# Attention and squared-ReLU MoE on one core: loading w_out once, with a scale for each of its rows

## The chip, the cores and the metric

The kernel runs on one core of a Trainium2 chip (trn2). The metric is the device time of one execution in microseconds (us), lower is better. Before the change the runs gave a median of 1171.84 us (3 runs, 1171.61 to 1176.66).

## The reference, cut to what matters

```python
# q, k, v: (8, 8, 576, 64) float32; w_in (512, 2048), w_out (2048, 512), both float64
scores = (1 / np.sqrt(64)) * np.matmul(q, k.transpose(0, 1, 3, 2))
mask = block_i >= block_j                       # blocks of 64 positions
scores = np.where(mask, scores, -1000000000.0)
scores = scores - np.max(scores, axis=-1, keepdims=True)
attn = np.exp(scores)
attn = attn / (np.sum(attn, axis=-1, keepdims=True) + 1e-09)
attn_out = np.matmul(attn, v)
x = attn_out.transpose(0, 2, 1, 3).reshape(4608, 512)
h = x @ w_in
r = np.maximum(h, 0.0)
return ((r * r) @ w_out).astype(np.float32)
```

## The kernel before, in words

**Attention.** The 8 heads of each of 8 batches are taken in 4 pairs. A "pass" is one pair on some of its 9 blocks of 64 queries. Passes 0 to 7 do the first three blocks of batches 0 and 1, passes 8 to 11 the other six blocks of batch 0, passes 12 to 15 those of batch 1, and passes 16 to 39 all nine blocks of batches 2 to 7. A pass computes the scores (`ps`, L406), the softmax (`nmx`, `p`, `rs`, `p_rows`, L425 to L456), turns the probabilities (`p_turned`) and multiplies them by v (`px`, L537). Up to pass 11 TensorE turns them (`pt`, L486, evicted at L488); from pass 12 on two DMA transposes for each pass do (L459, queued on SyncE), into one buffer, and probabilities and v are split into two f16 parts (`p_rows` z = 0 and 1, L454 and L455; `v`, L377 and L378).

**MoE.** The tokens go in 12 chunks of 384. A chunk has 16 hidden units `ph` of 12 matmuls each (`moe_in`, L685), whose relu (`r`, L692) is squared into an f16 pair (`g`, L694 to L696), and three outputs `po` of 48 matmuls each (`moe_out`, L711, 144 in all), evicted to `ob` (L719) and stored. TensorE's f16 products need each float64 weight as a scaled f16 pair `w1h`, `w1l` (w_in) and `w2h`, `w2l` (w_out).

**The weights.** The 16 tiles of w_in (512 KB each) are loaded once, early on; `weight_scale(0)` takes a maximum over each group of 4 tiles, and `weight_parts(0)` makes the pair. For w_out, `weight_scale(1)` loads all 16 tiles (named `wa`), reduces each to a maximum for every partition (L265) and then takes one maximum over all; after that `weight_parts(1)` loads all 16 tiles a second time (named `wb`) and splits them: ScalarE's Prelu (L305), VectorE's shift and or (L307, L308), ScalarE's cast to `w2h` (L309), GpSimd's rest to `w2l` (L310). All these tiles take their buffers from the ring of three that the q and k tiles of the passes use too (tag `qk32`, L218).

**What sets the order.** The program emits one pass after another (`one_pass`) and between the groups of a pass pours in steps of generators (`fill`): `first_moe` for chunk 0, then `moe` for each chunk that is complete. In `first_moe` one step is a hidden unit, together with a tile of w_in's parts and, from unit 8 on, one `wa` tile; when the 16 units are out, `wb` tiles and then `moe_out` follow. `load` of the pass after next stands at the end of a pass, `load_v` three passes ahead, into a ring of four `vraw` buffers. All loads, stores and transposes are issued by SyncE in one queue (SP). The tile scheduler then moves instructions of one engine by its own estimate, so that each engine's final order is not that of the code.

Of the kernel before, what the change touches and what calls it, by code (L numbers as in the profile page):

```python
# [58 lines left out]
BP = 99  # L59
BS = 99  # L60
# [39 lines left out]
def attention_moe_kernel(ctx: ExitStack, tc: tile.TileContext, qkt, vm, vt, w_in, w_out, out):  # L100
# [16 lines left out]
    vraw = [const.tile([P, 2, 5, D], F32, name=f"vraw{i}") for i in range(4)]  # L117
# [120 lines left out]
    gate = {}  # L238

    wsc = [const.tile([P, n], F32, name=f"wsc{i}") for i, n in enumerate((NG, 1))]  # L240
    wm = const.tile([P, NG], F32, name="wm")

# [13 lines left out]
    def weight_scale(wi):  # L256
# [3 lines left out]
        tok, ng = ((tokA, NG), (tokB, 1))[wi]  # L260
        st = small.tile([P, NF], F32, tag="stw", name=f"stw_{wi}", bufs=1)
        n = NF // ng
        for f in range(NF):
            _, _, hf = load_w(w_out, f, f"wa{wi}_{f}") if wi else w1raw[f]
            i = nc.vector.tensor_reduce(st[:, f : f + 1], hf, axis=AX.X, op=ALU.max, apply_absolute_value=True)  # L265
            if wi == 0 and f >= BS and (1, 0) in gate:
                behind(i, gate[1, 0])
            if f % n == n - 1:
                q = f // n
                st1 = small.tile([P, 1], F32, tag="st1", name=f"st1_{wi}_{q}", bufs=1)  # L270
                nc.vector.reduce_max(st1, st[:, f + 1 - n : f + 1], axis=AX.X)
                m = pow2_of_max(st1, 1, f"w{wi}_{q}", 2.0**-27, wm[:, q : q + 1] if wi == 0 else None)
                s = wsc[wi][:, q : q + 1]
                nc.vector.tensor_scalar(
                    s.bitcast(I32), m.bitcast(I32), -1, (127 + W_TOP) << 23, op0=ALU.mult, op1=ALU.add
                )
            yield
        if wi == 0:
            m = small.tile([P, 1], F32, tag="m", name="m_w")
            nc.vector.reduce_max(m, wm, axis=AX.X)  # L280
# [3 lines left out]
        if wi == 0:  # L284
            nc.vector.tensor_scalar(tokA, tokA, 2.0 ** (A_X + A_W - 1), None, op0=ALU.mult)
            inv = scale_of(m, 0, 1, "w")
            nc.vector.tensor_scalar(wm, wm, inv, None, op0=ALU.mult)
            nc.vector.tensor_tensor(wm, wm, wm, op=ALU.mult)
        else:
            nc.vector.tensor_scalar(tokB, tokB, tokA, None, op0=ALU.mult)  # L290
            nc.vector.tensor_scalar(wm, wm, wsc[1], None, op0=ALU.mult)

    def weight_parts(wi):

        wh, wl = ((w1h, w1l), (w2h, w2l))[wi]
        for f in range(NF):
            wlo, whi, hf = load_w(w_out, f, f"wb{wi}_{f}") if wi else w1raw[f]
            if WT:
                t = p1.tile([P, 512], F32, tag=("qs", "k1", "k2")[(wi + f) % 3], name=f"wt{wi}_{f}")
            else:  # L300
                t = p2.tile([P, 512], F32, tag="r", name=f"wt{wi}_{f}", bufs=3)
# [344 lines left out]
    def first_moe(ck, firsts):  # L646
# [4 lines left out]
        while True:  # L651
# [266 lines left out]
```

## Time and profile before

| what | value |
|---|---|
| median of 3 runs | 1171.84 us (1171.61 to 1176.66) |
| profiled execution | 1173.53 us, span 1171.7 us |
| mean granted TensorE clock | 0.955 of full speed |
| TensorE busy | 1058.3 us, 90% of the span |
| VectorE, ScalarE, GpSimd busy | 642.5, 581.7, 313.5 us |
| TensorE busy from 100 to 220 us | 86.91 of 120 us, clock 0.86 |
| w_out loads | 16 of `wa` and 16 of `wb`, 512 KB each |

Times are in microseconds from the start of the span; PE is TensorE, DVE VectorE, ACT ScalarE, POOL GpSimd, SP SyncE's queue. "Idle before, releaser" is the time in which an engine stood in front of an instruction and what ended it. The profiled execution is 1.7 us above the median, and all sums below are made against the profiled one.

### The profile page before, as it was taken

How to read it: one execution, taken by the hardware profiler on the slowest of the kernel's cores; microseconds unless marked ns; L12 is line 12 of the kernel's file. 1: busy time of each engine (PE TensorE's matmuls, PEld its weight loads, DVE VectorE, ACT ScalarE, POOL GpSimd, SP SyncE). 2: the span in 40 equal slices, each digit the busy share in tenths (PEclk: the TensorE clock that was granted, in tenths of full speed). 3: DMA queues.
4: the chain of work that ended last, by engine and by line, in shares of the span. 5: the costliest groups of instructions: out<-in, count | busy, mean ns of one | idle time of the engine just before them, and what ended most of it. 6: DMA issues, size and time to landing. Idle time of an engine off the chain costs nothing. (4 is left out here: it accounts for less than half of the span.)

```text
span 1171.7 us, 19118 instructions
## 1 busy us (share of the span) xinstructions
PE 1058.3 (90%) x7212; PEld 535.8 (46%) x7212; DVE 642.5 (55%) x1607; ACT 581.7 (50%) x1444; POOL 313.5 (27%) x292
## 2 busy tenths in 40 slices
PE   6578676888989999999999899998999999999998
PEld 4234332344445445445444445444544545555453
DVE  6984574766667756655737844765675513212120
ACT  5685563476357726724726624744854622313140
POOL 0663144122202222231303311330240314313030
PEclk8679887989999999999999899999999999999999
DMA  9345457775565465724715444545456140000000
GB/s 319 126 133 159 143 152 228 168 151 121 109 147 124 102 141 127 141 74 92 148 43 118 100 98 109 123 90 117 95 110 115 26 77 18 10 18 1 27 1 27
DMA packets 260572, 123.92 MB, mean 106 GB/s; under 512 B 233344, under 2 KB 245632, under 8 KB 260480
## 3 DMA queue, kind: packets, MB, share of 16 engines
q1 hardware_dynamic: 260480, 122.71, 44.2%
q8 instruction: 56, 0.92, 0.3%
q14 instruction: 36, 0.29, 0.1%
HBM read 58.20 MB, written 9.44 MB: 58 GB/s over the span
## 5 line engine op out<-in xcount | busy, mean ns | idle before, releaser
L685 PE MATMUL ph<-xt,w1h 128*128 128x384 f16 x1536 | 382.7, 332 | 5.0 <-ACT r L692 4.3
L711 PE MATMUL po<-w2h,g 128*128 128x512 f16 x1152 | 357.9, 385 | 12.2 <-ACT w2h L309 9.4
L695 POOL TENSOR_TENSOR r<-r 128x384 f32<-128x384 f32 x192 | 173.5, 905 | 635.7 <-ACT g L694 608.2
L711 PEld LDWEIGHTS <-g 128*128 128x128 f16 x1728 | 166.0, 99 | 225.7 <-issue 42.5
L685 PE MATMUL ph<-xt,w1l 128*128 128x384 f16 x768 | 253.4, 330 | 0.0
L431 ACT ACTIVATE p<-ps,nmx 128x192 f32<-128x192 f32 (+8 forms) x288 | 148.6, 524 | 192.1 <-DVE nmx L428 166.3
L711 PE MATMUL po<-w2l,g 128*128 128x512 f16 x576 | 221.8, 385 | 4.9 <-POOL w2l L310 4.8
L685 PEld LDWEIGHTS <-w1h 128*128 128x128 f16 x1536 | 145.2, 99 | 119.5 <-issue 30.7
L455 DVE SCALAR_TENSOR_TENSOR p_rows<-p,rs,p_rows 128x320 f16<-128x320 f32 (+8 forms) x240 | 148.4, 654 | 48.9 <-ACT p_rows L454 48.6
L696 DVE TENSOR_TENSOR g<-r,g 128x384 f16<-128x384 f32 x184 | 113.4, 618 | 101.7 <-POOL r L695 101.7
L692 ACT ACTIVATE r<-ph 128x384 f32<-128x384 f32 x192 | 93.4, 488 | 152.5 <-PE ph L685 151.4
L406 PE MATMUL ps<-qk 64*64 64x384 f32 (+5 forms) x960 | 126.3, 503 | 16.8 <-ACT p L431 14.7
L454 ACT ACTIVATE p_rows<-p,rs 128x320 f16<-128x320 f32 (+8 forms) x240 | 120.9, 567 | 32.8 <-DMA p_turned<-p_rows 18.4
L425 DVE TENSOR_REDUCE nmx<-ps 128x1 f32<-128x192 f32 (+8 forms) x288 | 124.5, 480 | 20.5 <-PE ps L406 20.4
L694 ACT ACTIVATE g<-r 128x384 f16<-128x384 f32 x192 | 100.4, 523 | 3.8
L685 PEld LDWEIGHTS <-w1l 128*128 128x128 f16 x768 | 76.0, 99 | 51.5 <-issue 3.2
L537 PE MATMUL px<-p_turned,v 128*64 128x64 f16 (+2 forms) x1440 | 78.5, 257 | 19.8 <-DMA p_turned<-p_rows 16.0
L719 DVE TENSOR_SCALAR ob<-po,uv 128x512 f32<-128x512 f32 x36 | 28.9, 806 | 119.6 <-PE po L711 119.6
L537 PEld LDWEIGHTS <-v 128*64 128x64 f16 x1440 | 56.0, 114 | 58.5 <-DMA p_turned<-p_rows 23.3
L619 POOL TENSOR_TENSOR x<-x,hb 128x768 f32<-128x768 f32 (+1 forms) x16 | 42.7, 2669 | 78.8 <-DVE hb L610 62.5
L545 ACT ACTIVATE x<-px,xsc 128x384 f32<-128x384 f32 (+1 forms) x52 | 26.0, 506 | 75.6 <-PE px L537 65.3
L406 PEld LDWEIGHTS ps<-qk 64*64 64x64 f32 x960 | 37.4, 136 | 52.0 <-issue 21.5
(106 smaller groups left out, 721.6 us busy)
## 6 DMA issues: line engine op xcount, KB each, us to landing
qk<-in_qkt SPq DMA_DIRECT2D x32, 576.0 KB, 4.1
vraw<-in_vm SPq DMA_DIRECT2D x32, 256.0 KB, 3.8
wa<-in_w_out SPq DMA_DIRECT2D x16, 512.0 KB, 4.0
wb<-in_w_out SPq DMA_DIRECT2D x16, 512.0 KB, 4.5
out<-ob SPq DMA_DIRECT2D x32, 256.0 KB, 2.0
w1raw<-in_w_in SPq DMA_DIRECT2D x8, 512.0 KB, 7.3
w2h<-in_w_in SPq DMA_DIRECT2D x4, 512.0 KB, 11.3
w2l<-in_w_in SPq DMA_DIRECT2D x4, 512.0 KB, 10.3
```

The lines of the kernel that those rows point to most:

```text
L406: mm = nc.tensor.matmul(ps[rs, o : o + D * (c1 - c0)], q, k, start=True, stop=True)
L425: nc.vector.tensor_reduce(nmx[:, i : i + 1], ps[:, off : off + w], axis=AX.X, op=ALU.max, negate=True)
L431: nc.scalar.activation(p32[:, off : off + w], ps[:, off : off + w], AF.Exp, bias=nmx[:, i : i + 1], scale=es, accum_out=sm[:, i : i + 1],)
L454: nc.scalar.activation(hi, p32[:, off : off + w], AF.Copy, scale=rs[:, i : i + 1])
L455: nc.vector.scalar_tensor_tensor(lo, p32[:, off : off + w], rs[:, i : i + 1], hi, op0=ALU.mult, op1=ALU.subtract)
L537: nc.tensor.matmul(dst, t["v32"][:, h, c, :] if whole else t["v16"][:, zv, h, c, :], rhs, start=(c == 0 and pi == 0 and k == 0), stop=(c = ...
L685: mm = nc.tensor.matmul(ph[:, :CH], w[:, f, P * cc : P * cc + P], xt[:, z, cc, :], start=(i == 0), stop=(i == 11))
L692: nc.scalar.activation(r, ph[:, :CH], AF.Relu, scale=c)
L694: nc.scalar.activation(g[:, 0], r, AF.Square)
L695: nc.gpsimd.tensor_tensor(r, r, r, op=ALU.mult)
L696: (nc.gpsimd if f < G_POOL and ck < G_CK else nc.vector).tensor_tensor(g[:, 1], r, g[:, 0], op=ALU.subtract)
L711: mm = nc.tensor.matmul(po, gs[f][:, z, P * t : P * t + P], w[:, f, :], start=(i == 0), stop=(i == 3 * NF - 1))
```

## The change

w_out is loaded once. `w_out_parts` takes a tile, reduces it to a maximum for each partition (so for each row of w_out), makes a power-of-two scale of that row and splits the tile at once. The tiles take their buffers from the ring of two with tag `first`, which earlier holds the q and k of four of the first passes. The steps begin at hidden unit 8 (`W2_0`), and the separate 16 steps of the maxima are gone. When all 16 tiles are split, `w_out_scales` takes the maximum over all rows (for the factor of the output) and makes two tables: `gsc`, by which chunk 0's 16 `g` tiles are multiplied in place on VectorE, and `rsc`, which from chunk 1 on is the scale of the relu. For chunk 0 the relu's scale is `hsc`, one for each group of w_in. The `vraw` ring goes from four to three buffers, and the load of v moves from three passes ahead at the end of a pass to two passes ahead behind its first group.

```diff
-    vraw = [const.tile([P, 2, 5, D], F32, name=f"vraw{i}") for i in range(4)]
+    vraw = [const.tile([P, 2, 5, D], F32, name=f"vraw{i}") for i in range(3)]
...
-    def load_w(src, f, name):
-        raw = p2.tile([P, 512], I64, tag="qk32", name=name, bufs=3)
-        nc.sync.dma_start(raw, src[f])
+    def load_w2(f):
+        raw = p2.tile([P, 512], I64, tag="first", name=f"w2raw{f}")
+        nc.sync.dma_start(raw, w_out[f])
...
+    def to_parts(raw, scale, wh, wl, n):
+        wlo, whi, hf = raw
+        t = p1.tile([P, 512], F32, tag=("qs", "k1", "k2")[n % 3], name=f"wt{n}")
+        nc.scalar.activation(t, hf, AF.Prelu, scale=scale, alpha=-(2.0**32))
+        t = t.bitcast(I32)
+        nc.vector.tensor_scalar(t, t, 3, None, op0=ALU.logical_shift_left)
+        nc.vector.scalar_tensor_tensor(whi, wlo, 29, t, op0=ALU.logical_shift_right, op1=ALU.bitwise_or)
+        nc.scalar.copy(wh, hf)
+        nc.gpsimd.tensor_tensor(wl, hf, wh, op=ALU.subtract)
...
+    def w_out_parts():
+        for f in range(NF):
+            raw = load_w2(f)
+            m = w2m[:, f : f + 1]
+            nc.vector.tensor_reduce(m, raw[2], axis=AX.X, op=ALU.max, apply_absolute_value=True)
+            nc.vector.tensor_scalar(m.bitcast(I32), m.bitcast(I32), EXPMASK, None, op0=ALU.bitwise_and)
+            s = small.tile([P, 1], F32, tag="s", name=f"s_w2_{f}")
+            nc.vector.tensor_scalar(
+                s.bitcast(I32), m.bitcast(I32), -1, (127 + W_TOP) << 23, op0=ALU.mult, op1=ALU.add
+            )
+            to_parts(raw, s, w2h[:, f], w2l[:, f], NF + f)
+            yield
+
+    def w_out_scales():
+        st1 = small.tile([P, 1], F32, tag="st1", name="st1_o", bufs=1)
+        nc.vector.reduce_max(st1, w2m, axis=AX.X)
+        m = pow2_of_max(st1, 1, "w_o", 2.0**-27)
+        descale(tokB, m)
...
-            for _ in range(SCN if n >= SC0 else 0):
-                if next(scale, 0) is None:
-                    yield
-            if n == PT0:
-                yield from scale
-            for _ in range(PTN if n >= PT0 else 0):
+            if n >= W2_0:
                 if next(parts, 0) is None:
                     yield
             n += 1
-        for gen in (scale, parts):
-            yield from gen
+        yield from parts
+        w_out_scales()
+        for f, g in enumerate(gs):
+            nc.vector.tensor_scalar(g, g, gsc[:, f : f + 1], None, op0=ALU.mult)
         yield from moe_out(ck, gs)
...
-            nc.scalar.activation(r, ph[:, :CH], AF.Relu, scale=c)
+            sc = rsc[:, f : f + 1] if ck else hsc[:, f * NG // NF : f * NG // NF + 1]
+            nc.scalar.activation(r, ph[:, :CH], AF.Relu, scale=sc)
...
             if gi == 0 and i + 1 < len(passes):
                 front(passes[i + 1])
+                if i + 2 < len(passes):
+                    if passes[i - 1]["whole"]:
+                        hurry(lambda n, g: n < i)
+                    load_v(passes[i + 2])
...
                 load(passes[i + 2])
-                for n in range(i + 3, min(i + 4, len(passes))):
-                    load_v(passes[n])
```

How the order moves. On SP, in the middle of the w_out loads, before the change (`wa1_f` and `wb1_f` are the two loads of tile f, `vraw` and `qk32` loads of the passes, p_turned the transposes of pass 12):

```order
L218 DMA wb1_4_1473<-in_w_out 128x512
L218 DMA wb1_5_1490<-in_w_out 128x512
L350 DMA vraw0_80<-in_vm 128x2x256
L218 DMA wb1_6_1498<-in_w_out 128x512
L459 DMA_TRANSPOSE p_turned_89<-p_rows_88 128x30x128
L218 DMA wb1_7_1536<-in_w_out 128x512
L218 DMA wb1_8_1544<-in_w_out 128x512
L459 DMA_TRANSPOSE p_turned_89<-p_rows_88 128x30x128
L218 DMA wb1_9_1552<-in_w_out 128x512
```

And with the change, from tile 7 to pass 12's transposes (`w2raw` is the one load of a tile, `ob_0_t` an output of chunk 0):

```order
L213 DMA w2raw7_1347<-in_w_out 128x512
L371 DMA qk32_1_2_3_1959<-in_qkt 128x1152
L382 DMA vraw0_80<-in_vm 128x2x256
L384 DMA vraw0_80<-in_vt 64x2x64
L213 DMA w2raw8_1359<-in_w_out 128x512
...
L213 DMA w2raw15_1500<-in_w_out 128x512
L382 DMA vraw1_81<-in_vm 128x2x256
...
L752 DMA out_0<-ob_0_2_1839 128x512
L371 DMA qk32_2_0_0_2335<-in_qkt 128x1152
L491 DMA_TRANSPOSE p_turned_87<-p_rows_86 128x30x128
```

Tile 8's load now stands behind a load of v into `vraw0`, and pass 12's two transposes, which stood between `wb1_6` and `wb1_9`, stand behind chunk 0's last output.

On VectorE with the change, at the end of w_out's tiles (`w2m` holds the rows' maxima, `st1_o` to `m_w_o` the maximum over all rows, `g_0_f` the hidden units of chunk 0):

```order
L319 TENSOR_REDUCE w2m_113<-w2raw15_1500 128x1
L320 TENSOR_SCALAR w2m_113<-w2m_113 128x1
L322 TENSOR_SCALAR s_w2_15_1504<-w2m_113 128x1
L330 TENSOR_REDUCE st1_o_1516<-w2m_113 128x1
L181 TENSOR_REDUCE mx_w_o_1520<-pm_w_o_1518 1x1
...
L193 TENSOR_SCALAR m_w_o_1527<-pn_w_o_1525 128x1
L285 TENSOR_SCALAR tokB_109<-m_w_o_1527 128x1
L292 TENSOR_TENSOR gsc_115<-w2m_113,m_w_o_1527 128x16
...
L343 TENSOR_SCALAR gsc_115<-gsc_115 128x16
L702 TENSOR_SCALAR g_0_0_692<-g_0_0_692,gsc_115 128x768
```

Chunk 0's first output matmul, which before needed only w_out's first split tile, now stands behind the reduce of tile 15, the maximum over all rows and the multiplication of `g_0_0`.

On TensorE the first output matmuls of chunk 0 before (`po_0_t` is output t), taken up as the tiles came:

```order
L711 MATMUL po_0_0_1655<-w2h_108,g_0_0_693 128x512
L711 LDWEIGHTS g_0_0_693
L711 MATMUL po_0_1_1818<-w2h_108,g_0_0_693 128x512
L184 MATMUL pm_1_0_3_1483<-ident_99,st_1_0_3_1481 1x128
L711 LDWEIGHTS g_0_0_693
L711 MATMUL po_0_0_1655<-w2l_109,g_0_0_693 128x512
```

And with the change:

```order
L179 MATMUL pm_w_o_1518<-ident_97,st1_o_1516 1x128
L191 LDWEIGHTS ones_bf_78
L191 MATMUL pn_w_o_1525<-dg_w_o_1523,ones_bf_78 128x1
L569 MATMUL px_0_2_3_1_1593<-p_turned_87,vraw1_81 64x384 x4
...
L518 MATMUL pt_29_1629<-ident_97,p_rows_86 128x128
L740 LDWEIGHTS g_0_0_692
L740 MATMUL po_0_0_1556<-w2h_106,g_0_0_692 128x512
L740 LDWEIGHTS g_0_0_692
L740 MATMUL po_0_0_1556<-w2l_107,g_0_0_692 128x512
```

The output t = 0 is no longer interleaved with t = 1, and 144 output matmuls follow one another with a few transposes and small matmuls between them. Counted over TensorE's order, at the `px` of pass 15 (`px_1_3_3_1`) 468 MoE matmuls stand ahead of it before, and 501 with the change; at the `px` of passes 13 and 14 it is 356 and 360, 420 and 420. In the last batch both orders have the same count again, and the last three chunks stand behind all passes in both.

## Rows read from the trace of the kernel before

**Rows 1.** The page's busy times and shares of the span, by engine.
```profile
PE 1058.3 (90%) x7212; PEld 535.8 (46%) x7212; DVE 642.5 (55%) x1607; ACT 581.7 (50%) x1444; POOL 313.5 (27%) x292
```
**Rows 2.** The chain that ended last, its end: start, length, engine, work, count.
```profile
1012.37 31.08 PE po L711 x144
1043.45 31.20 PE ph L685 x192
```
**Rows 3.** Stretches: length, busy us (count) of five engines, clock, DMA share, GB/s.
```profile
100.00:220.00 120.00, 86.91 (x489) 39.40 (x488) 71.76 (x164) 62.53 (x128) 38.68 (x34) 0.86 0.57 164
```
**Rows 4.** TensorE's waits from 86 to 236: total us, times, longest.
```profile
PE pt L486 <- ACT p_turned L488: 10.7, 2, 9.3
PE po L711 <- ACT w2h L309: 9.4, 7, 3.6
```
**Rows 5.** TensorE in order of time: start, length, work, idle before and releaser.
```profile
120.84 1.86 PE L537 MATMUL px<-p_turned,vraw 128*64 128x384 f32 x24
...
136.42 1.97 PE L486 MATMUL pt<-ident,p_rows 128*128 128x128 f32 x8 [9.33 <-ACT p_turned L488]
...
151.90 1.06 PE L711 MATMUL po<-w2h,g 128*128 128x512 f16 x2
```
**Rows 6.** The tiles `wa`: durations min/median/max (ns), waits, landing.
```profile
L265 DVE TENSOR_REDUCE stw<-wa x16: 670/686/687, 71.6 to 127.4; 128x1 f32<-128x512 f32 x16
...
  DMA wa<-in_w_out: 23.6, 12
...
DMA to landing us min/median/max: 3.6/4.0/5.0
```
**Rows 7.** The tiles `wb`, in the same view.
```profile
L305 ACT ACTIVATE wt<-wb,wm x16: 747/758/787, 148.3 to 204.5; 128x512 f32<-128x512 f32 x16
L308 DVE SCALAR_TENSOR_TENSOR wb<-wb,wt x16: 681/693/694, 149.6 to 207.9; 128x512 int32<-128x512 int32 x16
L309 ACT CAST w2h<-wb x16: 635/650/679, 150.6 to 208.7; 128x512 f16<-128x512 f32 x16
L310 POOL TENSOR_TENSOR w2l<-wb,w2h x16: 1138/1338/1738, 151.4 to 209.4; 128x512 f16<-128x512 f32 x16
...
DMA to landing us min/median/max: 3.6/4.5/5.6
```
**Rows 8.** SyncE's queue in order of time: two `wb` issues.
```profile
189.41 1.46 SPq L218 DMA_DIRECT2D wb<-in_w_out  x2
```
**Rows 9.** Groups of VectorE by form, whole span: count, busy us, mean ns.
```profile
L307 DVE TENSOR_SCALAR wt<-wt 128x512 int32<-128x512 int32 x32 | 19.7, 620 | 21.8 <-ACT wt L305 21.8
...
L620 DVE CAST xt<-x 128x768 f16<-128x768 f32 x6 | 3.8, 631 | 0.0
...
L198 DVE TENSOR_SCALAR m<-pn 128x1 f32<-128x1 f32 x28 | 4.2, 149 | 11.9 <-PE pn L196 11.8
```
**Rows 10.** SyncE's queue: outputs of chunk 0 and pass 13's transposes.
```profile
214.53 1.91 SPq L723 DMA_DIRECT2D out<-ob  x3
...
220.86 5.87 SPq L459 DMA_TRANSPOSE p_turned<-p_rows  x1
...
227.55 4.60 SPq L459 DMA_TRANSPOSE p_turned<-p_rows  x1
```
**Rows 11.** The tile `p_turned`, whole span: how long its transposes took to land.
```profile
DMA to landing us min/median/max: 6.3/6.6/8.4
```
**Rows 12.** TensorE in order of time: the `px` of passes 13 and 15.
```profile
234.00 2.01 PE L537 MATMUL px<-p_turned,v 128*64 128x384 f16 x36 [1.21 <-DMA p_turned<-p_rows]
...
270.42 2.01 PE L537 MATMUL px<-p_turned,v 128*64 128x384 f16 x36 [0.37 <-DMA p_turned<-p_rows]
```
**Rows 13.** TensorE's waits from 270 to 1172: total us, times, longest.
```profile
PE px L537 <- DMA p_turned<-p_rows: 11.7, 9, 3.0
```
**Rows 14.** VectorE and GpSimd in order of time around 65 us.
```profile
65.09 1.65 DVE L308 SCALAR_TENSOR_TENSOR w2h<-w2h,wt 128x512 int32<-128x512 int32 x1
...
65.04 1.16 POOL L310 TENSOR_TENSOR w1l<-w2h,w1h 128x512 f16<-128x512 f32 x1 [5.61 <-ACT w1h L309]
```

More of the change, by code (lines that the diff above doesn't have):

```diff
@@ L237, in attention_moe_kernel @@
     w1raw = []
-    gate = {}
-    wsc = [const.tile([P, n], F32, name=f"wsc{i}") for i, n in enumerate((NG, 1))]
     wm = const.tile([P, NG], F32, name="wm")
+    wsc = const.tile([P, NG], F32, name="wsc")
+    hsc = const.tile([P, NG], F32, name="hsc")
+    w2m = const.tile([P, NF], F32, name="w2m")
+    rsc = const.tile([P, NF], F32, name="rsc")
+    gsc = const.tile([P, NF], F32, name="gsc")
+    C_BITS = (127 + 1 - A_X - A_W) << 23
     def load_w1(f, pool):
@@ L254, in load_w1, with weight_scale, descale @@
         w1raw.append(words(raw))
[L256 to L262, printed above, removed]
+    def weight_scale():
+        st = small.tile([P, NF], F32, tag="stw", name="stw", bufs=1)
+        n = NF // NG
         for f in range(NF):
[L264 to L267, printed above, removed]
+            nc.vector.tensor_reduce(
+                st[:, f : f + 1], w1raw[f][2], axis=AX.X, op=ALU.max, apply_absolute_value=True
+            )
             if f % n == n - 1:
                 q = f // n
-                st1 = small.tile([P, 1], F32, tag="st1", name=f"st1_{wi}_{q}", bufs=1)
+                st1 = small.tile([P, 1], F32, tag="st1", name=f"st1_{q}", bufs=1)
                 nc.vector.reduce_max(st1, st[:, f + 1 - n : f + 1], axis=AX.X)
-                m = pow2_of_max(st1, 1, f"w{wi}_{q}", 2.0**-27, wm[:, q : q + 1] if wi == 0 else None)
-                s = wsc[wi][:, q : q + 1]
+                m = pow2_of_max(st1, 1, f"w_{q}", 2.0**-27, wm[:, q : q + 1])
                 nc.vector.tensor_scalar(
-                    s.bitcast(I32), m.bitcast(I32), -1, (127 + W_TOP) << 23, op0=ALU.mult, op1=ALU.add
+                    wsc[:, q : q + 1].bitcast(I32), m.bitcast(I32), -1, (127 + W_TOP) << 23, op0=ALU.mult, op1=ALU.add
                 )
             yield
-        if wi == 0:
-            m = small.tile([P, 1], F32, tag="m", name="m_w")
-            nc.vector.reduce_max(m, wm, axis=AX.X)
+        m = small.tile([P, 1], F32, tag="m", name="m_w")
+        nc.vector.reduce_max(m, wm, axis=AX.X)
+        descale(tokA, m)
+        nc.vector.tensor_scalar(tokA, tokA, 2.0 ** (A_X + A_W - 1), None, op0=ALU.mult)
+        d = below(hsc, wm, m, NG)
+        nc.vector.tensor_scalar(d, d, -14 << 23, 8, op0=ALU.max, op1=ALU.mult)
+        nc.vector.tensor_scalar(d, d, C_BITS, 0, op0=ALU.add, op1=ALU.max)
+    def descale(tok, m):
         nc.vector.tensor_scalar(
@@ L283, in weight_scale @@
         )
[L284 to L295, printed above, removed]
-        for f in range(NF):
[L297 to L301, printed above, removed]
-            q = f * NG // NF
-            nc.scalar.activation(t, hf, AF.Prelu, scale=(wm if wi else wsc[0])[:, q : q + 1], alpha=-(2.0**32))
-            t = t.bitcast(I32)
-            nc.vector.tensor_scalar(t, t, 3, None, op0=ALU.logical_shift_left)
-            nc.vector.scalar_tensor_tensor(whi, wlo, 29, t, op0=ALU.logical_shift_right, op1=ALU.bitwise_or)
-            nc.scalar.copy(wh[:, f], hf)
-            nc.gpsimd.tensor_tensor(wl[:, f], hf, wh[:, f], op=ALU.subtract)
-            yield
@@ new lines, in w_out_scales @@
+    def w_out_scales():
[3 more added lines that the diff above has]
+        descale(tokB, m)
+        nc.vector.tensor_scalar(tokB, tokB, tokA, None, op0=ALU.mult)
+        d = below(gsc, w2m, m, NF)
+        r = rsc.bitcast(I32)
+        nc.vector.tensor_scalar(r, d, -28 << 23, 4, op0=ALU.max, op1=ALU.mult)
+        nc.vector.tensor_scalar(r, r, 127 << 23, None, op0=ALU.add)
+        by_group = rsc.rearrange("p (q f) -> p q f", q=NG)
+        nc.vector.tensor_tensor(
+            by_group, by_group, hsc[:, :, None].to_broadcast([P, NG, NF // NG]), op=ALU.mult
+        )
+        nc.vector.tensor_scalar(d, d, -15 << 23, 8, op0=ALU.max, op1=ALU.mult)
+        nc.vector.tensor_scalar(d, d, 127 << 23, None, op0=ALU.add)
@@ L323, in load_first @@
             t = p2.tile([P, 2, 2, T3], F32, tag="qk32", name=f"first{n}", bufs=3)
-        v = vraw[n]
+        v = vraw[n] if n < 3 else p2.tile([P, 2, 5, D], F32, tag="v16", name=f"firstv{n}")
         for c in range(2):
@@ L347, in load_v @@
         c = t["chunks"] = -(-t["keys"] // P)
-        v32 = t["v32"] = vraw[t["i"] % 4]
+        v32 = t["v32"] = vraw[t["i"] % 3]
         c4 = min(c, 4)
@@ L646, in first_moe @@
     def first_moe(ck, firsts):
-        scale, parts = weight_scale(1), weight_parts(1)
+        parts = w_out_parts()
         hidden = moe_in(ck)
```

22 lines of the change are left out of this document (11 added, 11 removed).

## The prediction

> **What bounds the kernel now.** First the page's busy times: TensorE is busy 1058.3 of 1171.7 us and no other engine above 55% [rows 1], so time is won only where TensorE stands still or is slowed. Next the end of the chain of waits: two of the last pure MoE blocks, 192 hidden matmuls in 31.20 us and 144 output matmuls in 31.08 us [rows 2], that is 0.1625 and 0.216 us for each. There TensorE has no gap; whatever the change wins must be won earlier and reach this tail as work already done. Then the table of stretches: from 100 to 220 us TensorE is busy 86.91 of 120 us at a mean granted clock of 0.86 [rows 3]. These 33 idle us are the largest hole, and it is the stretch in which w_out is loaded and split. The waits there name ScalarE's eviction of a turned block (10.7 us, one of them 9.3) and its cast to `w2h` (9.4 us in 7 waits) [rows 4]. In order of time chunk 0's first output matmul starts at 151.90 [rows 5], and the last of the 16 tiles is split at 209.4 [rows 7], so output matmuls trickle for almost 60 us behind the tiles.
>
> So the question is when the last tile is split after the change, since now nothing of chunk 0's output can start before it.
>
> **What goes.** Sixteen loads (`wa`, 4.0 us each to land) and the 23.6 us in which VectorE stood waiting for them, 12 times [rows 6]. The reduces stay (0.686 us each), now on the tiles that are also split. No matmul goes.
>
> **What is new: T0, the start of chunk 0's output.** Tiles 0 to 7 can be loaded and split beside the hidden units. Tile 8's load stands on SP behind a load into `vraw0`, and that buffer is free when `px` of pass 9 has read it. That `px` ran at 120.84 for 1.86 us [rows 5], hence issue at about 124. From there two buffers set the pace. A buffer's round: issue 0.7 (a pair took 1.46 [rows 8]), landing 4.5, reduce 0.69 [rows 6], two small operations 0.3 at 0.149 each [rows 9], then Prelu 0.76, shift 0.62, or 0.69, cast 0.65 and GpSimd's rest 1.34 [rows 7, 9], which is 4.1. Without any other wait that is 10.2 us for two tiles. Before, 16 tiles passed the last step between 151.4 and 209.4 [rows 7], 3.87 us each, with three buffers, so a round took 3 x 3.87 = 11.6 us: the engines take their instructions in order, and the reduces and evictions of the passes stand between. I take 11.5, near the measured round. Four rounds remain for tiles 8 to 15; the last starts 3 x 11.5 = 34.5 us after the first. Tile 15 is issued about 1.4 us after tile 14, lands after 4.5 and is reduced in 0.7. Then comes the maximum over all rows: some 14 small VectorE operations of 0.15 us [rows 9], two trips through TensorE and the first multiplication, which I put at 4 us. T0 = 124 + 34.5 + 1.4 + 4.5 + 0.7 + 4 = **169**; by the round of 10.2 it is 165, by 12 us 171, and 174 if every round of 12 has a landing of 5.6 [rows 7].
>
> **What the 16 multiplications of `g` cost.** None like them is in the trace. The nearest row by width is the cast of 128x768 from f32 to f16, 0.63 us [rows 9]; it could take as little as a small operation, 0.15 [rows 9], or, slowed by half by what GpSimd does beside it, 0.95. TensorE uses 3 x 0.216 = 0.65 us for each `g`, so at 0.63 they are just hidden behind the first output; at 0.95 they add 16 x 0.3 = 5 us. I take nothing, and the 5 us go into the range.
>
> **From T0 on.** The 144 output matmuls follow almost without a gap: 31.1 us [rows 2], and some 20 transposes of 0.165 us (8 in 1.97 at a lower clock [rows 5]) and one eviction, together 4. Before, the same matmuls took from 151.90 to about 227. The low clock after a stand can add up to 2 us here (two output matmuls took 1.06 us at 151.90 [rows 5] instead of about 0.6), within the range.
>
> But attention does not run on by itself. Pass 12's transposes now stand on SP behind the last output of chunk 0 and a load. The outputs' three issues took 1.91 us [rows 10]; with 0.8 for the eviction the first transpose is issued at T0 + 35.1 + 0.8 + 2.1 = T0 + 38. The first takes 5.87 and the second starts 6.7 to 7.1 later [rows 10] and lands after 6.6 [rows 11]: `px` of pass 12 at T0 + 51.7. Since `p_turned` is one buffer, pass 13 can turn only after that `px` (2.0 [rows 12]), with about 5 for the issues and 6.6 to land, 13.9 with small gaps: `px` of pass 13 at T0 + 65.6, of pass 14 at T0 + 79.5. Then TensorE is the bound: by the order 93 MoE matmuls (15.1 us), scores of about 4.3 us and a `px` of 2.0 come to 21.4, so `px` of pass 15 is at T0 + 101. With T0 = 169 these are 234.6 and 270, against 234.00 and 270.42 now [rows 12]: no later, although chunk 0's output came in one piece. And at that point 501 MoE matmuls are done instead of 468: 33 x 0.1625 = 5.4 us in hand. Together with 0.4 at pass 15 the gain is 5.8, or nearly 175 − T0. Parity is at T0 = 175.
>
> **What of it arrives.** After 270 TensorE waits 11.7 us in 9 waits for turned copies [rows 13]; with 33 matmuls fewer to cover them I expect one more, 1.3 us. The tail is the same in both orders. The `vraw` ring of three and the earlier v loads remove the 9.3 us stand at 136.42 [rows 5] as a stall of its own, but T0 is set by the tiles, so it is worth nothing here. The relu's scale becomes a column of a table instead of a constant; the instructions are as many as before, and ScalarE is no bound, so I take nothing.
>
> Sum: 1173.5 − 5.8 + 1.3 = 1169.0 for an execution like the profiled one, which is 1.7 above the median; so **1167** (rounded), 0.4% below the present median.
>
> **Rivals.** Each moves T0, and the time moves one to one with it.
>
> (1) *The chain starts earlier, faster.* The 23.6 us that VectorE stood behind `wa` loads [rows 6] also delayed the softmax of passes 8 and 9. Without them `px` of pass 9 may come up to 10 us sooner, so tile 8's load with it: T0 = 159, 1173.5 − 16 + 1.3 − 1.7 = 1157. For it: these waits fall into the same stretch. Against: TensorE fills that stretch with hidden units at full clock. Range 1152 to 1161.
>
> (2) *In-order waits on the new loads, slower.* VectorE now meets each reduce of `w2raw` in order as it met those of `wa`, where a wait cost 23.6/12 = 2.0 us [rows 6], and behind it stand the shift and or of the tile before, and the evictions of turned blocks for which TensorE waits. If each of the eight tiles 8 to 15 adds such a wait to the chain without waits, T0 = 165 + 16 = 181: 1173.5 + 6 + 1.3 − 1.7 = 1179. It decides from T0 = 175, and over 0.5% slower is from T0 = 181. For it: two buffers instead of three, and nothing of chunk 0 can start until the last tile, where now it could start with the first.
>
> (3) *VectorE and GpSimd slow each other.* Tiles 2 to 7 are split while GpSimd squares and subtracts for the hidden units. Beside a GpSimd subtraction the or took 1.65 us instead of 0.69 [rows 14, 7]. With six tiles that lose 1 us each and no slack before tile 8, T0 is 175: 1173.5 + 1.3 − 1.7 = 1173. Against: tiles 2 to 7 have room until 124. The Trainium skill, "SBUF — State Buffer", section "Who interferes with whom", says that a VectorE instruction with two SBUF inputs contends with a GpSimd instruction that reads SBUF, and that a reduce never does: the or would be slowed and the reduce not. By that rule, with which the trace agrees (1.65 against 0.69 us for the or), T0 would be 171 to 175 and the time 1169 to 1173.
>
> That the change does not do what its words say holds in part and in every case: for chunk 0 a maximum over all rows still comes first, ahead of the output rather than of the split.
>
> **How the numbers follow.** The forecast (T0 165 to 174, so 1163 to 1172, with the multiplications' 5 us up to 1177) gets 0.46, rival 1 0.22, rival 2 0.20, rival 3 0.12. A measurement of this kernel can tell about 0.5%, 5.9 us, from no change: faster is below 1166, slower above 1177.7. Of the forecast 0.20 falls below 1166, 0.24 between, 0.02 above; rival 1 is all faster, rival 2 all slower, rival 3 all the same. So faster 0.42, same 0.36, slower 0.22. The range runs from 1152 (rival 1's lower end) to 1181 (rival 2, T0 = 183); about one in ten lies on each side. The forecast by itself spans 1163 to 1174, most of it within 5 us of 1167.
>
> **What would show it.** In the new profile the first `po` of chunk 0 should start near 169 and the last end near 204; `px` of pass 12 near 221, of pass 13 near 235, of pass 15 near 270, with 501 MoE matmuls ahead of it. Between 125 and T0 TensorE should be nearly idle, with the wait ending on the maximum's small chain. The prediction is wrong if T0 is before 162 or after 176, if the reduces of `w2raw` show waits on their DMA of over 15 us in all (rival 2), if tile 8's load is issued well before 120 (rival 1), or if the multiplications of `g` take over 0.65 us and `po` waits for them.

## The result, and the profile after

The changed kernel takes 1179.34 us (median of 7 runs, 1178.95 to 1180.33) against 1174.08 us for the kernel before (7 runs). The ratio is 1.0049, 95% interval 1.0031 to 1.0067: slower by half a per cent. I had forecast 1167 against a median of 1171.84, so a ratio of 0.996 and a gain.

The page's busy times stand against [rows 1]: TensorE has as many instructions, VectorE 52 more, ScalarE as many that take a little longer, and the span is 6.4 us longer.

```profile
PE 1052.1 (89%) x7212; PEld 534.8 (45%) x7212; DVE 655.9 (56%) x1659; ACT 597.9 (51%) x1444; POOL 310.0 (26%) x291
```

The table of stretches, with the columns of [rows 3]: length, busy time of TensorE, its weight loads, VectorE, ScalarE and GpSimd, then TensorE's granted clock, the DMA share and GB/s.

```profile
100.00:220.00 120.00, 78.96 (x468) 38.46 (x460) 70.26 (x188) 52.16 (x110) 25.15 (x29) 0.80 0.35 97
220.00:300.00 80.00, 67.34 (x505) 35.49 (x506) 57.06 (x150) 53.80 (x133) 20.68 (x18) 0.93 0.72 148
...
140.00:160.00 20.00, 0.32 (x4) 0.14 (x4) 9.31 (x23) 5.13 (x8) 3.65 (x3) 0.50 0.34 113
```

In the stretch where TensorE was busy 86.91 us before [rows 3], it is now busy 78.96. From 140 to 160 it does next to nothing. From 220 to 300 it is idle for 12.7 us at a clock of 0.93.

TensorE's waits from 86 to 260 name the hole, against [rows 4] (which end at 236). The evictions and casts that led the list before no longer do, and two waits for VectorE stand in their place.

```profile
PE pm_w_o L179 <- DVE st_o L330: 26.1, 1, 26.1
PE pm L179 <- DVE st L394: 6.7, 1, 6.7
PE px L569 <- DMA p_turned<-p_rows: 5.6, 3, 2.7
```

TensorE in order of time, against [rows 5] and [rows 12]: start, length, work, and in brackets the idle time before it and what ended it.

```profile
139.84 0.48 PE L438 MATMUL ps<-qk,qz 128*64 128x64 f32 x4
166.38 0.37 PE L179 MATMUL pm_w_o<-ident,st_o 128*1 128x128 f32 x1 [26.05 <-DVE st_o L330]
...
168.58 4.59 PE L569 MATMUL px<-p_turned,vraw 128*64 128x384 f32 x28
173.09 0.33 PE L518 MATMUL pt<-ident,p_rows 128*128 128x128 f32 x1
173.26 0.38 PE L740 MATMUL po<-w2h,g 128*128 128x512 f16 x1
...
208.59 2.51 PE L569 MATMUL px<-p_turned,vraw 128*64 128x384 f32 x28
...
220.34 0.37 PE L179 MATMUL pm<-ident,st 128*1 128x128 f32 x1 [6.72 <-DVE st L394]
220.50 0.84 PE L634 MATMUL nq<-sq,ones_bf 128*128 128x384 bf16 x2
224.05 3.65 PE L569 MATMUL px<-p_turned,v 128*64 128x384 f16 x36 [2.71 <-DMA p_turned<-p_rows]
...
240.99 2.01 PE L569 MATMUL px<-p_turned,v 128*64 128x384 f16 x36 [1.08 <-DMA p_turned<-p_rows]
...
281.17 2.01 PE L569 MATMUL px<-p_turned,v 128*64 128x384 f16 x36 [1.48 <-DMA p_turned<-p_rows]
```

Read from the top. `pm_w_o` is the transpose of the maximum over all rows; it waits for the last tile's reduce. Behind it, in TensorE's order, stands the `px` of pass 10 (168.58), whose turned blocks were all evicted by 135.6. T0, chunk 0's first output matmul, is 173.26. The 144 output matmuls are over at 206.3, and only then come the last turned blocks and the `px` of pass 11 (208.59). Next TensorE stands 6.7 us at another `pm`, the maximum of pass 14's v. Behind that one stands `nq`, the sums of squares from which chunk 1's tokens are made. The `px` of pass 12 follows at 224.05, that of pass 15 at 281.17 against 270.42 before [rows 12].

The tiles, against [rows 6] and [rows 7] (durations min/median/max in ns; waits in us and times), and the multiplications of chunk 0's hidden units in the same view:

```profile
L319 DVE TENSOR_REDUCE w2m<-w2raw x16: 667/686/689, 44.0 to 165.2; 128x1 f32<-128x512 f32 x16
L304 DVE SCALAR_TENSOR_TENSOR w2raw<-w2raw,wt x16: 678/692/1259, 75.2 to 167.6; 128x512 int32<-128x512 int32 x16
...
  DMA w2raw<-in_w_out: 19.8, 11
...
L702 DVE TENSOR_SCALAR g<-g,gsc x16: 410/411/419, 170.8 to 175.7; 128x768 f16<-128x768 f16 x16
```

SyncE's queue: tile 8's load with the one after it, tile 15's, and the load of pass 14's v between pass 12's two transposes.

```profile
123.99 3.74 SPq L213 DMA_DIRECT2D w2raw<-in_w_out  x2
...
161.51 0.33 SPq L213 DMA_DIRECT2D w2raw<-in_w_out  x1
...
210.62 5.04 SPq L491 DMA_TRANSPOSE p_turned<-p_rows  x1
215.76 0.59 SPq L382 DMA_DIRECT2D vraw<-in_vm  x1
216.45 0.55 SPq L384 DMA_DIRECT2D vraw<-in_vt  x1
217.05 5.04 SPq L491 DMA_TRANSPOSE p_turned<-p_rows  x1
```

The buffer of pass 14's v is that of pass 11 (a ring of three), free at about 211.1, once the `px` at 208.59 has read it. By then the first of pass 12's transposes has been issued (210.62), and the load, behind it in the queue, follows at 215.76, some 4.7 us after its buffer is free.

### The profile page after: what moved, and what is told of

The parts are those of the page before. It is cut to its first block, busy times and chain, and to the rows that moved or that the text cites. A ratio compares the mean times of both kernels' runs of the same rounds, so it can differ in the third digit from the quotient of the medians.

```text
span 1178.1 us, 19140 instructions
## 1 busy us (share of the span) xinstructions
PE 1052.1 (89%) x7212; PEld 534.8 (45%) x7212; DVE 655.9 (56%) x1659; ACT 597.9 (51%) x1444; POOL 310.0 (26%) x291
## 5 line engine op out<-in xcount | busy, mean ns | idle before, releaser
L740 PE MATMUL po<-w2h,g 128*128 128x512 f16 x1152 | 352.9, 381 | 3.2 <-DVE g L725 2.1
L740 PE MATMUL po<-w2l,g 128*128 128x512 f16 x576 | 219.3, 381 | 0.0
L725 DVE TENSOR_TENSOR g<-r,g 128x384 f16<-128x384 f32 x184 | 119.1, 652 | 95.5 <-POOL r L724 95.3
L721 ACT ACTIVATE r<-ph,rsc 128x384 f32<-128x384 f32 x176 | 101.7, 578 | 132.0 <-PE ph L713 131.0
L487 DVE SCALAR_TENSOR_TENSOR p_rows<-p,rs,p_rows 128x576 f16<-128x576 f32 (+8 forms) x240 | 140.8, 627 | 49.5 <-ACT p_rows L486 49.4
L486 ACT ACTIVATE p_rows<-p,rs 128x576 f16<-128x576 f32 (+8 forms) x240 | 120.9, 566 | 61.3 <-PE pt L518 19.8
L438 PE MATMUL ps<-qk 64*64 64x384 f32 (+5 forms) x960 | 126.1, 499 | 21.9 <-ACT p L463 21.7
L471 DVE TENSOR_SCALAR sm<-sm 128x2 f32<-128x2 f32 (+2 forms) x104 | 26.3, 253 | 64.5 <-ACT p L463 63.9
```

The source lines that it names most:

```text
L438: mm = nc.tensor.matmul(ps[rs, o : o + D * (c1 - c0)], q, k, start=True, stop=True)
L486: nc.scalar.activation(hi, p32[:, off : off + w], AF.Copy, scale=rs[:, i : i + 1])
L487: nc.vector.scalar_tensor_tensor(lo, p32[:, off : off + w], rs[:, i : i + 1], hi, op0=ALU.mult, op1=ALU.subtract)
L721: nc.scalar.activation(r, ph[:, :CH], AF.Relu, scale=sc)
L725: (nc.gpsimd if f < G_POOL and ck < G_CK else nc.vector).tensor_tensor(g[:, 1], r, g[:, 0], op=ALU.subtract)
L740: mm = nc.tensor.matmul(po, gs[f][:, z, P * t : P * t + P], w[:, f, :], start=(i == 0), stop=(i == 3 * NF - 1))
```

## The experiments

Theory A was that the dropped steps were the loss: with 16 steps fewer in `first_moe`, `w_out_scales` is emitted before the `px` of pass 10 and stands ahead of it on TensorE. Rival B was that only T0 counts, rival C that the ring of three v buffers costs the time. Each ratio below is to the kernel before on the same chip, with its 95% interval.

**e1, sixteen empty steps put back.**

```diff
         yield from parts
+        for _ in range(16):
+            yield
         w_out_scales()
```

> The changed kernel, with 16 empty steps before the maximum over all rows, as many as the change dropped. TensorE's order then has the px of pass 10, all turned blocks of pass 11 and then the maximum's transpose (pm_w_o); the px of pass 11 comes right behind it and that of pass 12 among the output matmuls. Theory A (the px of pass 10 stands behind pm_w_o, which waits for the last tile, and so holds passes 11 to 15): the px of pass 10 starts before 145 instead of 168.6, that of pass 12 before 205 instead of 224, T0 stays within 3 us of 173, and the time falls by 8 to 16 us, to 1163 to 1171. Rival B (only T0, the start of chunk 0's output, counts): T0 and the time stay, 1176 to 1182. Rival C (the ring of three v buffers and the new place of its loads cost the time): stays, 1176 to 1182.

Measured: 1154.88 us, ratio 0.9821 (0.9795 to 0.9847), a larger gain than expected. In order of time on TensorE, the `px` of pass 10, `pm_w_o`, the `px` of pass 11 and 12 and the first output matmul:

```profile
134.15 4.12 PE L569 MATMUL px<-p_turned,vraw 128*64 128x384 f32 x28
171.64 0.37 PE L179 MATMUL pm_w_o<-ident,st_o 128*1 128x128 f32 x1 [10.22 <-DVE st_o L330]
173.70 4.75 PE L569 MATMUL px<-p_turned,vraw 128*64 128x384 f32 x28 [0.42 <-DVE m_w_o L193]
...
178.38 0.39 PE L742 MATMUL po<-w2h,g 128*128 128x512 f16 x1
...
199.64 2.01 PE L569 MATMUL px<-p_turned,v 128*64 128x384 f16 x36 [0.37 <-DVE mx L181]
```

T0 is 5 us later than in the changed kernel (I had expected it within 3), and the kernel is 24 us faster. So T0 alone does not rule, and what stands behind the wait does.

**e2, four steps.** The same edit with `range(4)`.

> The changed kernel, with only 4 empty steps there: the px of pass 10 and the first three of pass 11's seven turned blocks stand ahead of pm_w_o, the others and the px of pass 11 behind it. Theory A: px of pass 10 before 145, px of pass 11 hardly earlier than now (208.6) since it still stands behind all of chunk 0's output, so a gain of at most a third of that with sixteen steps: 1173 to 1178. Rivals B and C: 1176 to 1182.

Measured: 1173.71 us, 0.9976 (0.9961 to 0.9992), as theory A has it. The `px` of pass 10 is at 135.61, but that of pass 11 at 209.32, behind the output as before.

**e3, without the multiplications.**

```diff
-        for f, g in enumerate(gs):
-            nc.vector.tensor_scalar(g, g, gsc[:, f : f + 1], None, op0=ALU.mult)
```

> The changed kernel without the multiplication of chunk 0's hidden units by the rows' factors (left out, so chunk 0's rows of the output are computed with unmatched scales). The output matmuls of chunk 0 then wait for their own tiles and not for the maximum over all rows. The px of pass 10 still stands behind pm_w_o. Theory A: pm_w_o still at about 166 and the px of pass 10 at 168 or later, but chunk 0's output is nearly done by then, so the px of pass 11 comes at 180 to 190 instead of 208.6, and the time falls by 10 to 20 us, to 1159 to 1169. Rival B says about the same, since T0 falls to about 125. Rival C: stays at 1176 to 1182. If the time does not fall by over 5 us, the wait of the output for the last tile costs nothing and A and B are both wrong.

Measured: 1150.94 us, 0.9789 (0.9765 to 0.9813), a larger gain than expected. The first output matmul is at 123.57, the `px` of pass 10 still at 165.16, that of pass 11 at 187.72. So the output's wait for the last tile, which the change brings in for chunk 0, is dear as long as the passes stand behind that output. Rival B expected about the same here, so this run does not tell A from B.

**e4, the v part alone in the kernel before.**

```diff
-    vraw = [const.tile([P, 2, 5, D], F32, name=f"vraw{i}") for i in range(4)]
+    vraw = [const.tile([P, 2, 5, D], F32, name=f"vraw{i}") for i in range(3)]
...
+                if i + 2 < len(passes):
+                    if passes[i - 1]["whole"]:
+                        hurry(lambda n, g: n < i)
+                    load_v(passes[i + 2])
...
-                for n in range(i + 3, min(i + 4, len(passes))):
-                    load_v(passes[n])
...
-        load_v(passes[NT * NHP + 2])
```

> The kernel before with the v part of the change alone: a ring of three v buffers, loads two passes ahead behind the first group of a pass. Theory A and rival B: within 0.3% of the kernel before. Rival C: slower by 0.4% or more.

Measured: 1176.95 us, 1.0011 (0.9990 to 1.0032). In the order of the kernel before the v part costs nothing that can be measured. There the `px` of pass 11 is at 160.30, long before pass 14 needs its buffer.

**e5, the second loads of the kernel before in a ring of their own** (on top of e4's edit).

```diff
+        if name[1] == "b":
+            raw = p2.tile([P, 512], I64, tag="first", name=name)
+        else:
+            raw = p2.tile([P, 512], I64, tag="qk32", name=name, bufs=3)
```

> The kernel before, still with both loads of w_out, but the second ones take the ring of two that the first passes leave (as the changed kernel does) and not the ring of three that holds q and k; the v part of the change is in it to make room. Theory A2 (the kernel before lost time because q and k of pass 13 had to wait for a buffer held by a tile of w_out, so its px came at 234 although that of pass 12 was done at 205): the px of pass 13 before 222, and 1155 to 1168, so most of what sixteen steps gave (1155) is the ring and not the single load. Rival D (the second load itself costs, by its transfers and by the output matmuls that trickle behind them): px of pass 13 at 230 or later and 1170 to 1180.

Measured: 1176.57 us, 1.0015 (0.9997 to 1.0033), with the `px` of pass 13 at 240.89. Theory A2 is wrong and D fits. Its output matmuls trickle behind the second loads (they waited 16.4 us in 5 times for the cast to `w2h`) until 241, and the `px` of pass 13 stands behind them.

**e6, e1 with the tiles in the ring of q and k.**

```diff
-        raw = p2.tile([P, 512], I64, tag="first", name=f"w2raw{f}")
+        raw = p2.tile([P, 512], I64, tag="qk32", name=f"w2raw{f}", bufs=3)
```

> The changed kernel with the sixteen empty steps, but w_out's tiles in the ring of three of q and k, as before. Three buffers instead of two bring the last tile earlier: T0 at 158 to 170 instead of 178. The q and k of passes 12 to 15 stand behind all tiles on the queue. Theory A2 (a tile in the ring of q and k holds the passes): px of pass 12 later than 205 and of pass 13 later than 222, and 1158 to 1170 in spite of the earlier T0. Rival B (T0 counts): below 1150.

Measured: 1153.39 us, 0.9814 (0.9784 to 0.9845). T0 is 161.63 and the `px` of pass 12 and 13 at 192.11 and 216.47, so the shared ring holds nobody: A2 falls again. But 17 us of T0 go with 1.5 us of time in this order, so B falls too.

**e7, e1 with the tiles from hidden unit 0.** One line, `W2_0 = 0`. Begun there, w_out's parts are written over raw tiles of w_in that are not split yet, so part of the hidden units is computed from other weights; the work and its order on the engines are those of such a kernel.

> The changed kernel with the sixteen empty steps, and w_out's tiles begun at hidden unit 0 instead of 8. If the chain of tiles sets T0, T0 comes 5 us or more earlier than 178 and the time falls by about as much, to 1145 to 1152. If the hidden units are delayed by it (the same engines split w_in's tiles there), hidden units end later than 126 and nothing is gained: 1153 to 1162.

Measured: 1146.12 us, 0.9754 (0.9715 to 0.9793), T0 at 171.72. This is an estimate of what an earlier start would give, some 8 us, if the raw tiles of w_in had another place. That it is T0 which gives it is not shown: in e6 T0 was earlier still and gave 1.5 us.

**e8, thirty-two steps.** The edit of e1 with `range(32)`.

> The changed kernel with 32 empty steps: the px of passes 10 to 13 stand ahead of pm_w_o, so the attention is freer, and pm_w_o may wait for px and not for the last tile. Theory A: the px of passes 12 and 13 no later than with sixteen steps (199.6 and 214.3); whether the time falls depends on T0: if it stays within 5 us of 178, 1148 to 1156; if pm_w_o now waits for the px of pass 13, T0 goes beyond 195, and chunk 0's output is late, 1156 to 1168.

Measured: 1189.42 us, 1.0127 (1.0094 to 1.0161), above both expected ranges. Its rows of TensorE (`pm_w_o`, first output matmul), and a stretch in the columns of above:

```profile
210.48 0.27 PE L179 MATMUL pm_w_o<-ident,st_o 128*1 128x128 f32 x1
...
226.27 0.39 PE L742 MATMUL po<-w2h,g 128*128 128x512 f16 x1 [1.58 <-DVE g L704]
...
100.00:220.00 120.00, 70.24 (x476) 34.29 (x476) 88.63 (x227) 70.06 (x153) 32.29 (x31) 0.73 0.58 143
```

Now `pm_w_o` stands behind the `px` of pass 13, although the last tile is reduced at 176, and from 125 to 226 TensorE has no MoE matmul to put between the steps of attention: from 100 to 220 it is busy 70 of 120 us. So the order can be wrong both ways: in the changed kernel the passes stand behind the output, here the output behind the passes, and TensorE has too little to do in either.

**e9, the shared ring without steps.** The edit of e6 on the changed kernel itself.

> The changed kernel without empty steps, with w_out's tiles in the ring of three of q and k. T0 comes about 12 us earlier (e6 had 161.6), while in TensorE's order the px of pass 10 still stands behind pm_w_o and that of pass 11 behind all 144 output matmuls. If, as predicted, the time moves one to one with T0 in this order, 1165 to 1170. If T0 has as little weight as between e1 and e6 (17 us of T0, 1.5 us of time), 1175 to 1181. Then only what stands behind the output counts.

Measured: 1157.68 us, 0.9850 (0.9808 to 0.9892). T0 is 163.35, 9.9 us earlier than in the changed kernel, and the time falls by 21.7 us, twice as much as my one to one and not as little as the rival had it. Its TensorE, first output matmul, `px` of pass 11 and the sums of squares:

```profile
163.35 0.39 PE L740 MATMUL po<-w2h,g 128*128 128x512 f16 x1 [0.96 <-DVE g L702]
...
198.73 2.51 PE L569 MATMUL px<-p_turned,vraw 128*64 128x384 f32 x28
205.80 0.32 PE L634 MATMUL nq<-sq,ones_bf 128*128 128x384 bf16 x1
```

From the `px` of pass 11 to `nq` it takes 7.1 us here and 11.9 in the changed kernel; the longest stand for a maximum of v is 2.6 us instead of 6.7. The queue differs too. Pass 14's v still waits for the `px` of pass 11 to free its buffer, but its load (201.16) now stands ahead of pass 12's transposes:

```profile
201.16 0.56 SPq L382 DMA_DIRECT2D vraw<-in_vm  x1
...
202.47 9.57 SPq L491 DMA_TRANSPOSE p_turned<-p_rows  x2
```

**e10 and e11, twelve and twenty steps.** The edit of e1 with `range(12)` and `range(20)`.

> The changed kernel with 12 empty steps: the px of passes 10 and 11 stand ahead of chunk 0's output, but that of pass 12 behind 135 of its 144 matmuls (with sixteen steps behind 91). Theory A in its finer form (each px that gets ahead of the output is worth some microseconds, since the next pass's rows, transposes and softmax follow it): between four and sixteen steps, px of pass 12 at 205 to 215, time 1158 to 1170. If the px of pass 10 and 11 were all that counted, the same as sixteen steps: 1152 to 1157.

> The changed kernel with 20 empty steps: the px of pass 11 ahead of pm_w_o, those of passes 12 and 13 among the output matmuls (behind 39 and 98 of 144). If the order of px against output is the whole story, at least as good as sixteen steps: 1148 to 1156. If T0 now moves beyond 188 because pm_w_o waits for the px of pass 11 and the scores ahead of it, part of what thirty-two steps lost shows: 1156 to 1168.

Measured: 1152.36 us, 0.9805 (0.9763 to 0.9847) with twelve and 1160.75 us, 0.9886 (0.9838 to 0.9934) with twenty. With twelve the `px` of pass 12 is at 211.14, 11 us later than with sixteen, and the time is the same: the finer form of theory A is wrong, and the time is what was expected if only the `px` of passes 10 and 11 count. The order from pass 16 on is not what the steps gain by: ahead of the first `px` of pass 17 TensorE has 636 MoE matmuls in the kernel before and in e1, 660 in the changed kernel, and 660 in e10 too, which is as fast as e1. With twenty T0 is 185.66, not yet the 188 that I had named, and the time lies in the range of e8's loss beginning.

**e12, e1 without the multiplications** (the edits of e1 and e3 together).

> The changed kernel with sixteen empty steps and without the multiplication of chunk 0's hidden units (left out, as in e3), so the output matmuls take up tile by tile what is split, and the passes are ahead of pm_w_o as well. It prices the maximum that still comes first for chunk 0, once the order of the passes is mended: 1138 to 1147 if TensorE's hole between 125 and 178 was worth filling; 1150 to 1156 if the passes bound it and not chunk 0.

Measured: 1148.26 us, 0.9761 (0.9710 to 0.9812), between the two expectations. The medians put the maximum that still comes first for chunk 0 at 6 to 7 us in this order, but the intervals of e1 and e12 overlap, so the price is not shown.

**e13, pass 14's v in a buffer of its own,** in the changed kernel.

```diff
         v32 = t["v32"] = vraw[t["i"] % 3]
+        if t["i"] == 14:
+            v32 = t["v32"] = p2.tile([P, 2, 5, D], F32, tag="first", name="v_14")
+            nc.gpsimd.memset(v32[D:P, :, 4, :], 0.0)
```

> The changed kernel, only that the v of pass 14 is loaded into a buffer of its own (one of the ring that w_out's tiles have left) instead of the vraw buffer that the px of pass 11 has to free. TensorE's order up to the px of pass 12 is the same. In the changed kernel TensorE stood 6.7 us in front of the transpose of v's maximum for pass 14 (220.34), and behind it stood the sums of squares (nq) of batch 0, on which chunk 1's tokens wait. If that wait is a part of the loss: nq at 216 or earlier, chunk 1's first hidden unit 4 us or more before 229.4, and 1171 to 1175. If it only ran beside the wait for the transposes of pass 12 (px at 224.05): 1176 to 1181, and the loss is T0 and the order alone.

Measured: 1167.79 us, 0.9933 (0.9914 to 0.9952), clearly below the changed kernel's 1.0049 (1.0031 to 1.0067). TensorE's first output matmul, `px` of pass 11, the v maximum, `nq`, and the `px` of passes 12 and 15:

```profile
172.71 0.55 PE L743 MATMUL po<-w2h,g 128*128 128x512 f16 x1
...
208.44 2.51 PE L572 MATMUL px<-p_turned,vraw 128*64 128x384 f32 x28 [0.16 <-DVE p_turned L523]
...
214.34 0.37 PE L179 MATMUL pm<-ident,st 128*1 128x128 f32 x1
...
216.74 0.48 PE L637 MATMUL nq<-sq,ones_bf 128*128 128x384 bf16 x1 [1.72 <-DVE sq L621]
222.16 3.73 PE L572 MATMUL px<-p_turned,v 128*64 128x384 f16 x36 [4.94 <-DMA p_turned<-p_rows]
...
272.35 2.01 PE L572 MATMUL px<-p_turned,v 128*64 128x384 f16 x36 [0.99 <-DMA p_turned<-p_rows]
```

Up to the `px` of pass 11 the two kernels agree within 0.8 us. Then the `pm` no longer waits, and `nq` ends its wait 3.8 us sooner (216.74, where I had named 216). The `px` of pass 12 comes 1.9 us sooner; its two transposes are issued in one go at 210.48, since the load that lay between them is gone. Chunk 1's first hidden unit is at 227.78, only 1.6 us sooner and not 4, and yet the time is below the range that I gave for this case.

So the edit does more than take away one stand. It moves the order too: ahead of the `px` of pass 13 stand 382 MoE matmuls instead of 360, so that this `px` comes 0.9 us later (241.93) but with 22 matmuls more already done, worth 3.6 us at 0.1625 each. At the `px` of pass 15 the lead is 8.8 us with 9 matmuls fewer done, and at the first `px` of pass 17, with 660 ahead in both, it is 6.6 us. The rest of the 11.8 us of span comes at one place. Pass 17 in the changed kernel, and then in e13:

```profile
327.40 0.36 SPq L752 DMA_DIRECT2D out<-ob  x1
327.99 4.72 SPq L491 DMA_TRANSPOSE p_turned<-p_rows  x1
330.68 0.55 PE L569 MATMUL px<-p_turned,v 128*64 128x128 f16 x18
334.65 3.73 PE L569 MATMUL px<-p_turned,v 128*64 128x384 f16 x36 [3.43 <-DMA p_turned<-p_rows]
...
316.74 5.60 SPq L494 DMA_TRANSPOSE p_turned<-p_rows  x1
322.45 0.50 SPq L755 DMA_DIRECT2D out<-ob  x1
324.10 2.37 PE L572 MATMUL px<-p_turned,v 128*64 128x128 f16 x54
```

In the changed kernel the second transpose of pass 17 is issued behind a store of chunk 1's output, in e13 ahead of it. Behind this pass's `px` the lead is 11.9 us (the next scores are at 338.31 and 326.39), and to the end it stays between 10 and 13. So 6.6 us go with the v that comes in time and what follows from it up to pass 17, and 5.3 us with an order in pass 17 that the edit also changed; that the late v causes this order too is not shown. The 6.6 us alone are about the changed kernel's whole loss (5.3 us by the medians, 6.4 by the spans), and in this order rival C was right to that extent, though e4 shows nothing in the other. How they divide between the stand, the load between the transposes and the order is not told apart.

It is not the number of buffers as such. e9 has the ring of three, issues pass 14's v ahead of the transposes, has pass 17's transpose ahead of the store like e13, and reaches the `px` of pass 15 at T0 + 100.3, where e13 has T0 + 99.6 and the changed kernel T0 + 107.9. Between e13 and e9 T0 differs by 9.4 us and the ratio by 0.0083, 9.7 us: with that path mended the time moves about one to one with T0, as I had predicted, and the rest of e9's gain is the path.

**e14 and e15, pairs of edits:** twelve steps with e6's shared ring, and twelve steps with e13's buffer.

> Twelve empty steps and w_out's tiles in the ring of three of q and k, the two edits that helped most for their size. If they mend the same thing (the px of passes 10 and 11 behind the wait for the last tile), together about what the better one gives, 1149 to 1156. If T0 and the order are separate losses, 1140 to 1147.

> Twelve empty steps and pass 14's v in its own buffer. With px of pass 11 at about 176 its buffer is free long before, so the own buffer should be worth nothing here: 1150 to 1155 as with twelve steps alone. If it still gives 3 us or more, the wait for v is a loss of its own.

Measured: 1152.45 us, 0.9810 (0.9785 to 0.9835) and 1155.99 us, 0.9839 (0.9812 to 0.9867). Neither adds to twelve steps alone. The own buffer gives nothing where the `px` of pass 11 is early, which fits that e13's gain hangs on that `px` being late; and steps and ring seem to mend the same loss.

**Which kernel is best.** With the steps put back, twelve to sixteen, the change is worth 1.8 to 2.0%: 1152 to 1155 us, faster than both kernels.

## Why the prediction was wrong, point by point

- **What bounds the kernel, and the tail.** Right for the tail: the last three chunks take the same time in both. The changed kernel and e13 keep a distance of 10 to 13 us from pass 18 on. Against the kernel before the distance is not steady: at the `px` of pass 15 the changed kernel is 10.75 us later with 33 MoE matmuls more (5.4 us), at that of pass 20 3.55 us with 15 more (2.4 us), at that of pass 35 5.55 us with as many. Why it shrinks and grows again there was not followed.
- **T0.** Forecast 169, measured 173.26, within the 165 to 174 of the text. Tile 8 was issued at 123.99 (forecast 124) and tile 15 at 161.51, 37.5 us later where the rounds gave 35.9. It landed sooner by 0.8, and the way from its reduce to the first multiplied `g` took 5.3 us where I had 4. The last 2 us are the `px` of pass 10 and a turned block, which stand between `pn_w_o` and the first output matmul and which I left out. T0 makes 4.3 us of the miss.
- **The multiplications.** 0.41 us each and hidden, as forecast (0.63 by the nearest row).
- **From T0 to pass 12.** Right: the first transpose at T0 + 37.4 (forecast 38), the `px` of pass 12 at T0 + 50.8 (51.7).
- **From pass 12 to 15.** Wrong. The `px` of pass 13 and 15 came at T0 + 67.7 and T0 + 107.9, forecast 65.6 and 101. The way from T0 to the `px` of pass 15 is 6.9 us too long, so parity was not at T0 = 175; with the measured T0 my own sum would have said about no change.
- **The step that failed** is the way from pass 12 to pass 15, and in it the sentence that the ring of three and the earlier v loads are "worth nothing here". The profiled execution took 1179.9 us where I had 1169.0; T0 makes 4.3 us of these 10.9 and this way 6.9. I looked at the stall that the new loads remove (9.3 us [rows 4]) and not at which `px` frees the buffer in the new order. It is that of pass 11, which the change puts behind chunk 0's whole output, and the load then stood behind a transpose in the queue. Pass 14's v came late, and chunk 1's sums of squares stood behind its maximum on TensorE. With that v in time e13 has the `px` of pass 15 at T0 + 99.6 with 492 MoE matmuls done; the 9 that it lacks to 501 make it T0 + 101.1, and I had forecast 101. That e13's time, 1167.79, lies within 1 us of the forecast is luck in part: e13 gains 5.3 us in pass 17, which my sum does not have, and its T0 is 172.71 and not 169.
- **What of it arrives.** Luck. From the distance at pass 15 my sum gives 10.75 - 5.4 + 1.3 = 6.7 us of loss, and the span is 6.4 us longer. But the waits for turned copies from there on did not grow by the 1.3 us that I took. They grew by 8.8, from 11.7 in 9 times [rows 13] to the 20.5 in the line below, while others shrank: those of `iv` for `m` are 2.1 instead of 6.9 us and those of `ps` for `p` 4.8 instead of 8.9.

```profile
PE px L569 <- DMA p_turned<-p_rows: 20.5, 13, 3.4
```

- **What I read but did not price.** The order of TensorE that I quoted has the `px` of pass 10 behind `pm_w_o`. I took the stand in front of it as idle time with nothing to do. e1 and e10 show that the work was there: 24 and 27 us below the changed kernel.
- **Rival 2** had the sign and the time, 1179, but not the mechanism. Its mark was met (19.8 us of waits on the tiles' DMA, over 15), yet T0 was 173 and not 181. e1 has such waits too, 15.5 us, and is fast.
- **Rivals 1 and 3.** Tile 8 did not come earlier. The or was slowed only now and then, 1.26 us at most against a median of 0.69.

## What to carry to other kernels

Where the order of a program is poured out in steps, dropping steps moves everything that comes after them: first put the count back, then judge the change. On an engine that takes its instructions in order, look at what is ready and stands behind a wait for something global, and at the last reader of each buffer in the new order, before a smaller ring is called free. Two per cent lay here in where a single small transpose stands: with twelve or sixteen steps ahead of it 1152 to 1155 us, with none 1179, with thirty-two 1189. And an edit that frees one buffer can move the order of every engine behind it, so follow the lead along the trace before its whole gain is put down to that buffer.

## What the runs showed of the hardware

TensorE's granted clock was 0.50 of full speed, its lower level of 1.2 GHz, in the stretch in which it stood (140 to 160 us), and the work after a stand pays: the `px` of pass 10 took 4.59 us at 168.58 (clock 0.52 from 168 to 173) and the `px` of pass 11 with as many matmuls 2.51 at 208.59 (1.00 from 208 to 212), that of pass 12 3.65 (0.57 from 224 to 228) and that of pass 13 2.01 (1.00 from 240 to 244). A hole on TensorE thus cost more here than its own length. The multiplication of 128x768 f16 by a column took 0.41 us, where the cast of as many elements from f32 took 0.63 [rows 9].
